# Spreading output products over the steps of a banded-attention kernel, with the early conv and value work and the first diagonals reordered

## The chip, the cores and the metric

One core of one Trainium2 chip. The metric is the device time of one execution in microseconds (us), lower is better. A run counts as slow if it is more than 1.5% above the fastest of its kernel; ratios use the other runs. The experiments ran on different chips, so compare kernels of different tables by their ratios.

Engine names as in the profile: PE is the matrix engine (TensorE), PEld its weight loads, DVE VectorE, ACT ScalarE, POOL GpSimd, SP the engine that issues most transfers (SPq is its queue).

## The reference

Inputs q, k, v are 8 x 8 x 576 x 64. Heads 0 to 3 attend to the last 32 positions, heads 4 to 7 to every fourth of the last 128. The result goes through a gated unit.

```python
scores = scale * np.matmul(q, k.transpose(0, 1, 3, 2))
mask_plain = (rel >= 0) & (rel < window)                       # heads 0..3
mask_dil = (rel >= 0) & (rel < window * dilation) & (rel % dilation == 0)
...
x = np.ascontiguousarray(attn_out.transpose(0, 2, 1, 3)).reshape(B, S, H * D)
...
for k in range(K):                                             # K = 5, causal
    gate_pre += conv_w[k][None, None, :] * xp[:, k:k + S, :]
gate = 1.0 / (1.0 + np.exp(-gate_pre))
val = x @ w_val
return (gate * val @ w_out).astype(np.float32)
```

## The kernel before

The loop runs over 32 head pairs, called steps; four make one batch, two make one group (one load of k and q). In a step PE does the scores (two halves of six products), ScalarE the exp, VectorE the mask, PE the product with the values (two halves), VectorE the normalisation. Into its waits PE gets work of earlier steps: the transposes of the next k and q (`trans_main`, `trans_rest`), the transposed attention result (`trans_x`), the gate's convolution as products with diagonal matrices (`conv`), the value products (`val`) and the output products (`out_tile`). The order is the program's: the schedule is manual. In the program `NCH` is 4 and `EARLY` 7; `xn` is the normalised attention result, `xT` its transpose, `k_b`, `q_b`, `vA` and `vB` are bf16 copies of loaded tiles. What matters of it, with `[...]` for cuts:

```python
    def normalize(i):            # after both halves of the attention product
        [...]
        nc.vector.reciprocal(out=rec[0:R], in_=av[:, :, :, D])
        nc.vector.tensor_tensor(out=dst, in0=av[:, :, :, 0:D], in1=rec..., op=ALU.mult)

    def out_tile(n):             # O4: four products of 512 columns
        [...]
        osb = out_pool.tile([128, Dm], FP32, name="osb")     # 4 buffers
        nc.scalar.mul(out=osb, in_=ps, mul=0.5)
        [... nc.sync.dma_start(out=out..., in_=osb...)]

    quota = [0.0]
    def slot_out():              # 1.125 credits a step, an output product for each
        quota[0] += 1.125
        while quota[0] >= 1 and outs:
            out_tile(outs.pop(0))
            quota[0] -= 1
    def slot_val():              # where no value product is due, an output product
        if vals:
            run_val()
        elif outs:
            out_tile(outs.pop(0))
            quota[0] -= 1

    for i in range(NP):
        [... loads]
        prep_v(i + 1)                                  # GpSimd: vA, vB
        [... cast(g2, "k"/"q", ..., nc.gpsimd)]        # GpSimd: k_b, q_b of a later group
        if i == NCH:                                   # the break at pair four
            after_x(i - 1); pop_conv(i + 1); pop_conv(i + 1)
            for _ in range(4): run_val()
            next_pair(i - 1); run_val(); run_val()
        scores(i, 0); scores(i, 1)
        [... after_x(i - 1), transposes, apply_mask(i, 0)]
        slot_val()
        pop_conv(...); apply_mask(i, 1); attn_v(i, 0)
        pop_conv(...); attn_v(i, 1); normalize(i)
        [... trans_rest]
        if i < NCH - 1: make_conv_diag(i + 1); warm(2)
        if i > NCH: slot_out()
        if vals: run_val()
```

An output product becomes due only when four value products more are done, that is in every second step, and then two or three at once; by then the credits for them have piled up. So from step 10 on two output products come after each even step (three in steps 12, 20 and 28) and none after an odd one. (`slot_val` spends credits in steps 5 to 7 alone, where no value product is due.) `warm(n)` are products of nothing, 512 columns, to keep PE busy.

The softmax here doesn't subtract the row's maximum and nothing guards it: scores larger than these inputs give would overflow.

Of the kernel before, what the change touches and what calls it, by code (L numbers as in the profile page):

```python
# [11 lines left out]
ALU = mybir.AluOpType  # L12
# [11 lines left out]
def kernel(  # L24
# [11 lines left out]
    nc = tc.nc  # L36

    B, H, S, D = q.shape
# [160 lines left out]
    def load_pair(g, a):  # L199
# [4 lines left out]
            load_rest(g, "q", nc.sync)  # L204
        load_v(g, a, a + 2)

    warm_in = consts.tile([1, 1], FP32, name="warm_in")
    nc.vector.memset(warm_in, 0.0)
    load_main(0, "k", 0, 2, nc.sync)
# [15 lines left out]
        out=ident, in_=ident, compare_op=ALU.not_equal, fill=1.0,  # L225
        base=0, pattern=[[-1, 128]], channel_multiplier=1,
    )
    nc.gpsimd.dma_start(out=conv_nat, in_=moe_conv_w)
    for kt in kTs:
        nc.vector.memset(kt[:, :, 0:KOFF], 0.0)  # L230
    for et in ets:
# [6 lines left out]
    def band(dst, pattern, base):  # L238
# [9 lines left out]
            channel_multiplier=1,  # L248
        )

    nc.gpsimd.memset(ident5, 0.0)
    nc.gpsimd.affine_select(
        out=ident5, in_=ident5, compare_op=ALU.not_equal, fill=1.0,
        base=0, pattern=[[-1, 8]], channel_multiplier=1,
    )
    band(mask_p[:, 1, :].rearrange("p (r t) -> p r t", r=4), [[1, 4], [4, 24]], 32)
    nc.gpsimd.tensor_copy(mask_p[:, 2:NB, :], mask_p[:, 1:2, :].to_broadcast([128, NB - 2, 96]))
    nc.gpsimd.tensor_copy(mask_p[:, 0, :], mask_p[:, 1, :])
# [31 lines left out]
    def finish_mask_d():  # L290
        mb = mask_d[:, 2 * TM:HB].rearrange("p (w t) -> p w t", w=2)
        nc.vector.tensor_scalar(
            out=par_i, in0=par_i, scalar1=1, scalar2=None, op0=ALU.bitwise_and)
        nc.vector.tensor_copy(same, par_i)
        nc.vector.tensor_tensor(
            out=mb, in0=mb, in1=same[:, :, None].to_broadcast([128, 2, TR]), op=ALU.mult)

    def setup_conv_w():
        ps = bank()
        for c in range(NCH):  # L300
            nc.tensor.transpose(
                out=ps[:, c * 8:c * 8 + K], in_=conv_nat[:, c * 128:(c + 1) * 128],
                identity=ident5[0:K, 0:K],
            )
        nc.scalar.copy(
            out=conv_w_sb, in_=ps[:, 0:NCH * 8].rearrange("p (c e) -> p c e", c=NCH)[:, :, 0:K])

    def make_conv_diag(c):
        nc.vector.tensor_tensor(
            out=conv_diag[:, c, :, :],  # L310
            in0=ident[:, None, :].to_broadcast([128, K, 128]),
            in1=conv_w_sb[:, c, :, None].to_broadcast([128, K, 128]),
            op=ALU.mult)
# [48 lines left out]
    def trans_rest(g):  # L362
        dil = g % 2
        t = grp_tiles[g]
        ps = bank_b()
        for z in range(2):
            nc.tensor.transpose(  # L367
                out=ps[:, 0, TM * z:TM * z + TM],
                in_=hi_bf16(t["rest"][:, 128 * z:128 * z + 128]), identity=ident)
        pv = ps[:, 0, 0:256].rearrange("p (z n) -> p z n", z=2)  # L370
        if not dil:
            if "qT" not in t:
                t["qT"] = qt_pool.tile([128, 2, DIL, T], BF16, name="qT")
            t["kT"] = kTs[(g // 2) % NKT]
            nc.vector.tensor_copy(t["kT"][:, :, KOFF + RM:KOFF + S], pv[:, :, 0:64])
            nc.vector.tensor_copy(
                t["qT"][:, :, :, TM:T], pv[:, :, 64:128].rearrange("p z (t r) -> p z r t", r=DIL))
        else:
            t["qB"] = qt_pool.tile([128, 4, 2, TR], BF16, name="qB")
            if "kB" not in t:  # L380
                t["kB"] = qt_pool.tile([128, 4, 64, 2], BF16, name="kB")
            nc.vector.tensor_copy(
                t["kB"][:, :, TM - TB:64, :],
                pv[:, :, 0:64].rearrange("p w (t h) -> p h t w", h=4))
            nc.vector.tensor_copy(
                t["qB"], pv[:, :, 64:128].rearrange("p w (t h) -> p h w t", h=4))
# [148 lines left out]
    def out_tile(n):  # L535
        ps = bank()
        for c in range(NCH):
            nc.tensor.matmul(  # L538
                out=ps, lhsT=y_all[:, c, 128 * n:128 * n + 128], rhs=w_out_b[:, c, :],
                start=(c == 0), stop=(c == NCH - 1),  # L540
            )
        osb = out_pool.tile([128, Dm], FP32, name="osb")
        nc.scalar.mul(out=osb, in_=ps, mul=0.5)  # L543
        p = 0
        while p < 128:
            f = 128 * n + p
            b, r, t = f // S, (f % S) // T, f % T
            w = min(128 - p, T - t)
            nc.sync.dma_start(
                out=out[b].rearrange("(t r) n -> r t n", r=4)[r, t:t + w, :],  # L550
                in_=osb[p:p + w, :])
            p += w
# [5 lines left out]
    def run_val():  # L558
        item = vals.pop(0)
        while item not in gates:  # L560
            conv(*convs.pop(0)[1])
        val(*item)
        done_val[0] += 1

        while HB * (done_val[0] // NCH) >= 128 * (done_out[0] + 1):
            outs.append(done_out[0])
            done_out[0] += 1

    def pop_conv(i):
        if convs and convs[0][0] < i:  # L570
            conv(*convs.pop(0)[1])

    def warm(n):
        for _ in range(n):
            nc.tensor.matmul(out=bank(), lhsT=junk[:, 0:128], rhs=junk, start=True, stop=True)
# [3 lines left out]
    def next_pair(i):  # L579

        j = i + 1
        g, z = j // 2, j % 2
        trans_main(g, "k", (z,))
        trans_main(g, "q", (z,))
        if z == 0:
            trans_rest(g)

    def after_x(i):
        b, c = pair_info(i)[0:2]
        trans_x(i)  # L590
        for G in range(2):
            convs.append((i + 1 + 0.5 * G, (b, c, G)))
        if c == NCH - 1:
            vals.extend((b, cc, G) for G in range(2) for cc in range(NCH))

    quota = [0.0]

    def slot_val():
        if vals:
            run_val()  # L600
        elif outs:
            out_tile(outs.pop(0))
            quota[0] -= 1

    def slot_out():
        quota[0] += 1.125
        while quota[0] >= 1 and outs:
            out_tile(outs.pop(0))
            quota[0] -= 1

    warm(8)
    cast(0, "k", 0, nc.vector)
    cast(0, "q", 0, nc.scalar)
    next_pair(-1)
    setup_conv_w()
    make_conv_diag(0)
    make_mask_d()
    make_perm()
    for i in range(NP):
        b, c, dil, g, a = pair_info(i)  # L620
        if i == 0:
            load_pair(2, 0)
        elif i == 1:
            load_pair(2, 2)
        elif i == 2:
            load_pair(3, 0)
        elif i == 3:
            load_pair(3, 2)
            load_group(4)
        if c % 2 == 0 and 5 <= g + 3 < 2 * B:  # L630
            load_group(g + 3)
        if i + 1 < NP:
            prep_v(i + 1)
        if i == 1:
            load_weight(w_val_b, moe_w_val)
        if i == 2:
            for name in ("k", "q"):
                cast(2, name, 0, nc.gpsimd)
        if i == 3:
            load_weight(w_out_b, moe_w_out)  # L640
            for name in ("k", "q"):
                cast(2, name, 2, nc.gpsimd)
        g2 = g + 2
        if 2 < g2 < 2 * B and g2 % 2 == 0:
            cast(g2, "k" if a == 0 else "q", 0, nc.gpsimd)
            cast(g2, "k" if a == 0 else "q", 2, nc.gpsimd)
        if i == NCH:
            after_x(i - 1)
            pop_conv(i + 1)
            pop_conv(i + 1)  # L650
            for _ in range(4):
                run_val()
            next_pair(i - 1)
            run_val()
            run_val()
        scores(i, 0)
        scores(i, 1)
        if i == 0:
            cast(0, "k", 2, nc.scalar)
            cast(0, "q", 2, nc.scalar)  # L660
        if i > 0 and i != NCH:
            after_x(i - 1)
        if NCH <= i < EARLY:
            next_pair(i)
        if i >= EARLY - 1 and g + 1 < 2 * B:
            trans_main(g + 1, "k" if a == 0 else "q")
        apply_mask(i, 0)
        if i < NCH:
            warm(3 if i == 0 else 1)
        slot_val()  # L670
        pop_conv(i if i >= NCH else i + 0.25)
        apply_mask(i, 1)
        attn_v(i, 0)
        if 0 < i < NCH - 1:
            next_pair(i)
        pop_conv(i + 0.5 if i >= NCH else i + 0.75)
        if i == 0:
            warm(1)
        attn_v(i, 1)
        normalize(i)  # L680
        if i == 0:
            next_pair(0)
            finish_mask_d()
        elif i >= EARLY - 1 and a == 0 and g + 1 < 2 * B:
            trans_rest(g + 1)
        if i < NCH - 1:
            make_conv_diag(i + 1)
            warm(2)
        if i > NCH:
            slot_out()  # L690
        if vals:
            run_val()
    pop_conv(NP)
# [38 lines left out]
```

## Time and profile before

Three runs: 192.55 us median (191.51 to 193.34). The profiled execution took 190.94 us, its span 189.2. A step ends where VectorE begins the reciprocal of the normalisation (L452); read from VectorE's timeline:

| end of step | 0 | 3 | 5 | 6 | 9 | 31 |
|---|---|---|---|---|---|---|
| us | 9.16 | 23.90 | 38.72 | 43.84 | 57.68 | 171.47 |

From step 9 on, two steps take 10.20 us (4.52 to 4.59 into an even step, 5.61 to 5.68 into an odd one; leaving out steps 13, 21 and 29, each behind a third output product, and the last two). How the clock, the transfers and their rate ran, in 40 slices of the span:

```profile
PEclk9999999999999999999999999999999999999999
DMA  5999999999998999999999969999780404021345
GB/s 153 257 300 309 263 253 297 319 230 341 304 201 257 335 295 213 287 316 284 246 294 322 263 159 268 328 283 242 249 280 0 111 3 151 19 77 40 110 111 166
```

A 9 is 90% or more. The transfers are busy until 140 us, and still move from 159 to 341 GB/s. The clock row says less about the first microseconds than it seems to: the trace's clock records begin at 5.00 us, and where there is none the view takes the clock as full. The start on VectorE (start, duration, instruction, in brackets the idle time before it):

```profile
4.58 0.43 DVE L181 CAST k_b<-k_nat 128x512 bf16<-128x512 f32 x1 [2.13 <-DMA k_nat<-in_k_dram]
...
6.95 0.91 DVE L309 TENSOR_TENSOR conv_diag<-ident,conv_w_sb 128x640 bf16<-128x640 bf16 x1
...
9.16 0.23 DVE L452 RECIPROCAL rec<-ps_sc 96x12 f32<-96x12 f32 x1 [0.46 <-PE ps_sc L441]
```

The first k is cast as soon as it lands; the first diagonal (L309) comes behind the first transposes.

### The profile page before, as it was taken

The page shows a single profiled execution, that of the slowest core. Times are in us where ns is not written, and L with a number is a line of the kernel's source. Part 1 is how long each engine was busy: PE and PEld are TensorE (multiplying, and loading weights), DVE is VectorE, ACT ScalarE, POOL GpSimd, SP SyncE. Part 2 cuts the span into 40 slices and gives each one's busy share as a digit, 9 for nine tenths or more (in the row PEclk, how much of TensorE's full clock was granted, in tenths as well). Part 3 has the DMA queues.
Part 4 walks back from the last instruction along what each step waited for, and adds up shares of the span by engine and source line. Part 5 has one row for each costly group of instructions (what it writes and reads, how often), then busy time and mean ns, then how long its engine had stood idle before and what let it go on. Part 6 is the DMA issues. An engine that isn't in the chain of part 4 may idle for free.

```text
span 189.2 us, 5191 instructions
## 1 busy us (share of the span) xinstructions
PE 166.2 (88%) x2039; PEld 119.4 (63%) x2057; DVE 118.8 (63%) x282; ACT 123.2 (65%) x218; POOL 41.0 (22%) x88
## 2 busy tenths in 40 slices
PE   6877769788898989899898989898999989899990
PEld 2455547466677665677676766766777766666650
DVE  3677637765576575765757764768667565756420
ACT  3756625788777676767787776767776877563341
POOL 7414420180090045003500350027030000000000
PEclk9999999999999999999999999999999999999999
DMA  5999999999998999999999969999780404021345
GB/s 153 257 300 309 263 253 297 319 230 341 304 201 257 335 295 213 287 316 284 246 294 322 263 159 268 328 283 242 249 280 0 111 3 151 19 77 40 110 111 166
DMA packets 62632, 42.28 MB, mean 223 GB/s; under 512 B 31371, under 2 KB 57995, under 8 KB 62608
## 3 DMA queue, kind: packets, MB, share of 16 engines
q1 hardware_dynamic: 60976, 40.57, 79.9%
q0 software_dynamic: 1088, 1.06, 3.3%
q8 instruction: 16, 0.26, 0.6%
q10 hardware_dynamic: 544, 0.33, 0.6%
q14 instruction: 8, 0.07, 0.1%
HBM read 33.56 MB, written 9.44 MB: 227 GB/s over the span
## 4 chain that ended last, share of the span: by engine, by line
PE 77%; DVE 15%; DMA 2%; ACT 2%; issue 2%; ACTq 0%; DVEq 0%
PE ps_bank L508 21%; PE ps_bank L538 16%; PE ps_bank L523 13%; DVE xn L457 8%; PE ps_bank L332 7%; PE ps_sc L441 7%; PE ps_sc L411 5%; PE ps_bank L469 3%; DVE rec L452 2%; DMA q_nat<-in_q_dram 2%; PE ps_bank L482 2%; PE ps_bank L476 2%; ACT et L414 1%; DVE xT L484 1%; PE ps_bank L367 1%
## 5 line engine op out<-in xcount | busy, mean ns | idle before, releaser
L508 PE MATMUL ps_bank<-xT,conv_diag 128*128 128x288 bf16 (+1 forms) x384 | 49.9, 266 | 2.0 <-DVE xT L484 2.0
L414 ACT ACTIVATE et<-ps_sc 128x576 bf16<-128x576 f32 x64 | 40.0, 650 | 14.6 <-PE ps_sc L411 13.4
L529 DVE SCALAR_TENSOR_TENSOR y_all<-gate,ps_bank 128x288 bf16<-128x288 bf16 x64 | 28.9, 451 | 20.2 <-PE ps_bank L523 17.8
L523 PE MATMUL ps_bank<-xT,w_val_b 128*128 128x288 bf16 x256 | 41.0, 286 | 0.2 <-DVE xT L484 0.2
L516 ACT ACTIVATE gate<-ps_bank 128x288 bf16<-128x288 f32 x64 | 26.5, 415 | 20.2 <-PE ps_bank L508 19.8
L508 PEld LDWEIGHTS <-conv_diag 128*128 128x128 bf16 x384 | 32.0, 97 | 8.9 <-issue 1.6
L543 ACT ACTIVATE osb<-ps_bank 128x512 f32<-128x512 f32 x36 | 21.6, 600 | 18.9 <-PE ps_bank L538 17.4
L538 PE MATMUL ps_bank<-w_out_b,y_all 128*128 128x512 bf16 x127 | 32.8, 379 | 0.9
L457 DVE TENSOR_TENSOR xn<-ps_sc,rec 96x768 bf16<-96x768 f32 (+1 forms) x32 | 30.6, 956 | 1.1
L523 PEld LDWEIGHTS <-w_val_b 128*128 128x128 bf16 x256 | 23.0, 98 | 7.2 <-issue 0.2
L181 POOL CAST k_b<-k_nat 128x512 bf16<-128x512 f32 x14 | 9.3, 687 | 82.4 <-DMA k_nat<-in_k_dram 57.4
L452 DVE RECIPROCAL rec<-ps_sc 96x12 f32<-96x12 f32 (+1 forms) x32 | 7.4, 231 | 25.3 <-PE ps_sc L441 25.3
L441 PEld LDWEIGHTS <-et 128*128 128x128 bf16 x384 | 19.8, 97 | 5.1 <-DVE et L423 2.4
L538 PEld LDWEIGHTS <-y_all 128*128 128x128 bf16 x144 | 13.4, 98 | 13.8 <-DVE y_all L529 1.3
L484 DVE COPY xT<-ps_bank 128x576 bf16<-128x576 bf16 x32 | 14.6, 458 | 11.4 <-PE ps_bank L482 6.5
L423 DVE TENSOR_TENSOR et<-et,mask_p 128x576 bf16<-128x576 bf16 x32 | 15.6, 494 | 0.5 <-ACT et L414 0.5
L423 DVE TENSOR_TENSOR et<-et,mask_d 128x576 bf16<-128x576 bf16 x32 | 15.6, 499 | 0.0
L188 POOL CAST vA<-v_st 128x512 bf16<-128x512 f32 x16 | 10.3, 641 | 16.9 <-DMA v_st<-in_v_dram 16.9
L411 PE MATMUL ps_sc<-qA,kA 64*128 64x128 bf16 x128 | 8.2, 219 | 6.3 <-DVE xn L457 4.8
L411 PE MATMUL ps_sc<-qT,kT 64*128 64x96 bf16 x192 | 8.2, 205 | 4.7 <-DVE xn L457 3.6
L441 PE MATMUL ps_sc<-vP,et 128*128 128x65 bf16 x192 | 11.3, 194 | 0.9 <-DVE et L423 0.8
L411 PEld LDWEIGHTS <-kA 64*128 64x128 bf16 x128 | 3.9, 94 | 11.4 <-DVE xn L457 5.9
(82 smaller groups left out, 190.6 us busy)
## 6 DMA issues: line engine op xcount, KB each, us to landing
k_nat<-in_k_dram SPq DMA_DIRECT2D x12, 512.0 KB, 5.6
q_nat<-in_q_dram SPq DMA_DIRECT2D x12, 512.0 KB, 6.4
vP<-in_v_dram SPq DMA_DIRECT2D x6, 768.0 KB, 8.4
v_st<-in_v_dram SPq DMA_DIRECT2D x6, 512.0 KB, 5.6
k_nat<-in_k_dram SPq DMA_DIRECT2D x8, 256.0 KB, 5.2
out_dram<-osb SPq DMA_DIRECT2D x8, 256.0 KB, 5.3
q_nat<-in_q_dram SPq DMA_DIRECT2D x7, 256.0 KB, 4.8
out_dram<-osb SPq DMA_DIRECT2D x8, 224.0 KB, 3.4
```

The lines of the kernel that those rows point to most:

```text
L411: nc.tensor.matmul(out=o, lhsT=lhsT, rhs=rhs, start=True, stop=True)
L414: nc.scalar.activation(out=e3, in_=ps[:, :, 0:HB], func=AF.Exp, scale=scale)
L423: nc.vector.tensor_tensor(out=e3, in0=e3, in1=m, op=ALU.mult)
L441: nc.tensor.matmul(out=ps[:, hf, x * AVS:x * AVS + D + 1], lhsT=et[:, hf, sl * HB + col:sl * HB + col + 128], rhs=rhs, start=True, stop=True)
L457: nc.vector.tensor_tensor(out=dst, in0=av[:, :, :, 0:D], in1=rec[0:R, :, :, None].to_broadcast([R, 2, 6, D]), op=ALU.mult)
L484: nc.vector.tensor_copy(xTs[b % NXT][:, c, :, 2:], pr)
L508: nc.tensor.matmul(out=ps[:, o * T:(o + n) * T], lhsT=conv_diag[:, c, K - 1 - m, :], rhs=xt[:, c, r:r + n, off:off + T], start=(idx == 0), ...
L516: nc.scalar.activation(out=gate, in_=ps[:, 0:HB], func=AF.Tanh, scale=0.5)
L523: nc.tensor.matmul(out=ps[:, 0:HB], lhsT=w_val_b[:, mc, c * 128:(c + 1) * 128], rhs=xt[:, mc, 2 * G:2 * G + 2, 2:], start=(mc == 0), stop= ...
L529: nc.vector.scalar_tensor_tensor(out=y_all[:, c, b * S + G * HB:b * S + (G + 1) * HB], in0=gates.pop((b, c, G)), scalar=1.0, in1=ps[:, 0:H ...
L538: nc.tensor.matmul(out=ps, lhsT=y_all[:, c, 128 * n:128 * n + 128], rhs=w_out_b[:, c, :], start=(c == 0), stop=(c == NCH - 1),)
L543: nc.scalar.mul(out=osb, in_=ps, mul=0.5)
```

## The change

Intent: (a) one output product in each step, so that each has enough PE work to cover its normalisation; (b) no burst of value products ahead of step 4: its work is spread like that of every other step, and the next pair's transposes go behind the first attention half; (c) the conv weights are transposed and the first three diagonals built at the very start, so that later steps need not. The diff, cut to its core:

```diff
+    nc.gpsimd.dma_start(out=conv_nat, in_=moe_conv_w)      # first of all, was after ident
 [...]
-        nc.scalar.copy(out=conv_w_sb, ...)
+        nc.vector.tensor_copy(conv_w_sb, ...)
 [... slot_val, slot_out, quota removed]
-    warm(8)
+    warm(5)
+    setup_conv_w()
+    make_conv_diag(0)
+    warm(3)
     cast(0, "k", 0, nc.vector)
     cast(0, "q", 0, nc.scalar)
-    next_pair(-1)
-    setup_conv_w()
-    make_conv_diag(0)
+    trans_main(0, "k", (0,))
+    make_conv_diag(1)
+    trans_main(0, "q", (0,))
+    trans_rest(0)
+    make_conv_diag(2)
 [... in the loop]
-        if i == NCH:
-            after_x(i - 1)
-            [... two convs, four vals, next_pair(i - 1), two vals]
-        if NCH <= i < EARLY:
-            next_pair(i)
-        if i >= EARLY - 1 and g + 1 < 2 * B:
+        if i >= EARLY and g + 1 < 2 * B:
             trans_main(g + 1, "k" if a == 0 else "q")
-        slot_val()
+        if vals:
+            run_val()
         attn_v(i, 0)
-        if 0 < i < NCH - 1:
+        if 0 < i < EARLY:
             next_pair(i)
+        if i == EARLY - 1:
+            trans_main(g + 1, "k")
 [... make_conv_diag(3) after step 0, none in the later steps]
-        if i > NCH:
-            slot_out()
+        for _ in range(2 if len(outs) > 2 else 1):
+            if outs:
+                out_tile(outs.pop(0))
```

More of the change, by code (lines that the diff above doesn't have):

```diff
@@ L227 @@
     )
-    nc.gpsimd.dma_start(out=conv_nat, in_=moe_conv_w)
+    nc.gpsimd.memset(ident5, 0.0)
+    nc.gpsimd.affine_select(
+        out=ident5, in_=ident5, compare_op=ALU.not_equal, fill=1.0,
+        base=0, pattern=[[-1, 8]], channel_multiplier=1,
+    )
     for kt in kTs:
@@ L249, in band @@
         )
-    nc.gpsimd.memset(ident5, 0.0)
-    nc.gpsimd.affine_select(
-        out=ident5, in_=ident5, compare_op=ALU.not_equal, fill=1.0,
-        base=0, pattern=[[-1, 8]], channel_multiplier=1,
-    )
     band(mask_p[:, 1, :].rearrange("p (r t) -> p r t", r=4), [[1, 4], [4, 24]], 32)
@@ L304, in setup_conv_w @@
             )
-        nc.scalar.copy(
-            out=conv_w_sb, in_=ps[:, 0:NCH * 8].rearrange("p (c e) -> p c e", c=NCH)[:, :, 0:K])
+        nc.vector.tensor_copy(
+            conv_w_sb, ps[:, 0:NCH * 8].rearrange("p (c e) -> p c e", c=NCH)[:, :, 0:K])
     def make_conv_diag(c):
@@ L594, in after_x @@
             vals.extend((b, cc, G) for G in range(2) for cc in range(NCH))
-    quota = [0.0]
-    def slot_val():
-        if vals:
-            run_val()
-        elif outs:
-            out_tile(outs.pop(0))
-            quota[0] -= 1
-    def slot_out():
-        quota[0] += 1.125
-        while quota[0] >= 1 and outs:
-            out_tile(outs.pop(0))
-            quota[0] -= 1
-    warm(8)
+    warm(5)
+    setup_conv_w()
+    make_conv_diag(0)
+    warm(3)
     cast(0, "k", 0, nc.vector)
     cast(0, "q", 0, nc.scalar)
-    next_pair(-1)
-    setup_conv_w()
-    make_conv_diag(0)
+    trans_main(0, "k", (0,))
[3 more added lines that the diff above has]
+    make_conv_diag(2)
     make_mask_d()
@@ L646 @@
             cast(g2, "k" if a == 0 else "q", 2, nc.gpsimd)
-        if i == NCH:
-            after_x(i - 1)
-            pop_conv(i + 1)
-            pop_conv(i + 1)
-            for _ in range(4):
-                run_val()
-            next_pair(i - 1)
-            run_val()
-            run_val()
         scores(i, 0)
@@ L660 @@
             cast(0, "q", 2, nc.scalar)
-        if i > 0 and i != NCH:
+        else:
             after_x(i - 1)
-        if NCH <= i < EARLY:
-            next_pair(i)
-        if i >= EARLY - 1 and g + 1 < 2 * B:
+        if i >= EARLY and g + 1 < 2 * B:
             trans_main(g + 1, "k" if a == 0 else "q")
@@ L682 @@
             next_pair(0)
+            make_conv_diag(3)
             finish_mask_d()
@@ L686 @@
         if i < NCH - 1:
-            make_conv_diag(i + 1)
             warm(2)
-        if i > NCH:
-            slot_out()
+        for _ in range(2 if len(outs) > 2 else 1):
+            if outs:
+                out_tile(outs.pop(0))
         if vals:
```

## The prediction

> **What bounds the kernel now.** I read the page first (engine shares, then the chain that ended last), then the chain in order of time through one pair of steady steps, then the waits, then the two stretches where the rhythm differs: the start, and the GpSimd casts around 37 us. A "step" is one head pair: scores, exp, mask, attention product, normalisation; there are 32, and the work of earlier pairs (transposes, gate convolution, value and output products) is threaded through them as filling.
>
> ```profile
> PE 166.2 (88%) x2039; PEld 119.4 (63%) x2057; DVE 118.8 (63%) x282; ACT 123.2 (65%) x218; POOL 41.0 (22%) x88
> ...
> PE 77%; DVE 15%; DMA 2%; ACT 2%; issue 2%; ACTq 0%; DVEq 0%
> ```
>
> PE is the engine that the end hangs on: 77% of the chain. What interests us is the 15% of VectorE: places where PE had run out of filling. The chain in order of time, steps 10 to 11:
>
> ```profile
> 62.33 1.67 PE ps_bank L538 x7
> 64.01 0.49 PE ps_bank L523 x4
> 64.50 0.37 PE ps_sc L411 x12
> ...
> 67.65 0.20 PE ps_sc L441 x6
> 67.86 0.02 issue
> 67.88 0.24 DVE rec L452
> 68.12 0.02 issue
> 68.15 0.97 DVE xn L457
> 69.11 0.05 issue
> 69.16 0.30 PE ps_sc L411 x6
> ```
>
> After the even step PE has two output products (L538) and a value product (L523) to do, and the scores (L411) run through without a wait. After the odd step it has one value product only: the chain leaves PE, goes through reciprocal and normalisation on VectorE, and returns 1.30 us later (67.86 to 69.16), since the second half of the scores needs the PSUM tile that the normalisation reads. The waits of PE:
>
> ```profile
> PE ps_sc L411 <- DVE xn L457: 8.4, 14, 0.7
> PE ps_sc L411 <- ACT et L414: 2.2, 3, 0.7
> PE ps_bank L508 <- DVE xT L484: 2.0, 4, 0.8
> ```
>
> In the timeline eleven of those 14 are the ends of the odd steps 9 to 29, 0.6 us each. The three waits on exp are steps 6, 7 and 8. So after step 9 the kernel is PE work plus 6.6 us of gaps. Before that, the end of step 3 (23.88 us) to the end of step 9 (57.65 us) is the stretch with the break at pair four. One row there matters later, from GpSimd's timeline:
>
> ```profile
> 37.07 1.64 POOL L181 CAST k_b<-k_nat 128x512 bf16<-128x512 f32 x2 [10.60 <-ACT kB L358]
> 38.66 0.61 POOL L188 CAST vA<-v_st 128x512 bf16<-128x512 f32 x1
> 39.22 0.40 POOL L191 CAST vB<-vB_st 128x256 bf16<-128x256 f32 x1
> ```
>
> The profile names an activation as releaser, but the program's waits on this cast are old ones except the load of k for group 4 (batch 2's first heads), which landed at 36.92 by the trace's semaphore records. It is a wait on DMA.
>
> **What the Trainium skill says.** "Perfetto Trace Analysis", Identifying the Most-Contended Engine: matmul busy share is a bad measure, since pipelined matmuls overlap in the trace; so I count PE time by the chain's pieces. The trace agrees: one L538 row lasts 379 ns, while four of them advance the chain by 0.86 us. "TensorE: Matmul & The Clock Gate", Wait — 56ns, not 53.3ns?: warm matmuls of 512 columns start every 215.7 ns; 0.86/4 = 0.215 us agrees, and granted clock is full in all 40 slices. The same page of trace analysis, Tensor Engine Instruction (MATMUL, LD_WEIGHTS), says that ScalarE, VectorE and GpSimd take their work strictly in order; the trace agrees, for the vA cast above starts only when the two k_b casts end although its own load had landed at 32.3. "DMA: Bandwidth & Descriptors", Specifications, puts HBM at about 358 GB/s per core; from 5 to 55 us my windows of 5 us show 258 to 316 GB/s with the DMA engines busy throughout, so I take it that early loads cannot come sooner.
>
> **The change part by part.** Instruction counts on PE are equal (the order listing shows 4109 rows in both, only moved), so everything is in the gaps.
>
> *Output products one per step.* Old order after an attention product: even steps O8 V4, odd steps V4 (O4 is one output tile's four matmuls, V4 one value product). New: every step O4 V4, O8 in steps 12, 20, 28. Needed cover: 1.30 us. New cover: O4 0.86 + V4 0.49 + first half of scores 0.18 to 0.25 = 1.53 to 1.60 us, plus 0.11 for the k/q rest transposes in even steps. That is over 1.30 in every step, by 0.2 to 0.4. Gaps removed: 11 x 0.6 = 6.6 us. Steps 9 to 31 last 171.44 - 57.65 = 113.8 us before, so 107.2 after; both do 25 output products in it.
>
> *No break, transposes behind the first half.* I rebuild steps 4 to 9 from the chain's pieces. Step 3 gains the transposes of the next pair (0.45 + 0.11), so it ends at about 23.88 + 0.56 = 24.4, plus what the start loses. Step 4: gap 1.30, second half of scores 0.27, x transposes 0.36, wait for xT 0.52, V4 0.49, attention 0.19, transposes 0.45, convolution 0.62, attention 0.19 = 4.4. Step 5 likewise 4.6 (no xT wait, one more convolution, rest transposes). So step 5 would end at 33.5 to 34.4. Step 6's first attention product would then be wanted at about 36.5 to 37.4. It reads vA and vB of pair 6, which GpSimd casts behind the k casts of group 4, which wait for a load landing at 36.9: vB is ready at 39.2 to 39.6 as before. This is the new wait, about 2 to 3 us. From there: remaining vB products 0.1, transposes 0.90, convolution 0.62, attention 0.19: step 6 ends at 41.3 (before: 43.8). Steps 7 to 9 are PE work, 4.83 each: rest transposes 0.11 or nothing, O4 0.86, V4 0.49, scores 0.37, x transposes 0.41, transposes 0.45, V4 0.49, two convolutions 1.24, two attention halves 0.38 = 4.7 to 4.8; the measured steps 10 and 11 give (10.26 - 0.6)/2 = 4.83. Step 9 ends at 41.3 + 14.5 = 55.8.
>
> *Start.* Building the diagonals earlier puts the weight copy and conv_diag ahead of the k cast on VectorE. conv_nat was issued at 1.53 and landed at 5.35; issued 0.7 earlier it lands near 4.6, the same time as k. Then transposes, copy (0.2) and conv_diag (0.82) come before the cast that ran at 4.58: the first pair's start is delayed by 0.4 to 1.3 us. In exchange diagonals 2 and 3 leave steps 1 and 2, where they ended just when VectorE was needed (16.70 against 16.72): nothing gained. But this loss ends in the wait of step 6, which hangs on a load and not on the start. On the path: 0.
>
> *Sum.* After the end of step 31 the tail is the same, except that one output product (0.86) is still owed. New end of step 31: 55.8 + 107.2 = 163.0, plus 0.86 = 163.9, against 171.44: 7.5 us. Time: 192.55 - 7.5 = 185.1 us, a ratio of 0.961.
>
> **The rivals.**
> First, no wait on the load: if vA is cast in time, step 6 ends 2 us sooner and the time is 183. Against it: GpSimd's order is the same in both builds, and up to 36.9 the loads are held up by the transfers ahead of them (the DMA row is full), not by compute.
> Second, DMA becomes the bound. A batch of four steps moves (33.56 MB read + 9.44 written - 2.1 of weights)/8 = 5.1 MB; at 4 x 4.83 = 19.3 us that asks 264 GB/s, near what the start shows at saturation. For it: the DMA row is at 9 until 140 us. Against it: in the steady part single slices reach 328 GB/s, loads are issued two to four steps before use, and the queue drains from 140 on. If it binds, half of the steady gain is lost: 188 to 189.
> Third, the gap does not close, because ScalarE or a bank takes the place of the normalisation: exp must now wait behind the copy of the output tile (0.60) in each step. ScalarE's load per step: two exp 1.3, copy 0.6, two gates 0.8, k/q copies 1.0 to 1.5 = 3.7 to 4.2 of 4.83. The first mask has slack of about 0.8 us before its attention product. If 0.2 us a step stays, 4 us are lost: 189.
> Fourth, the start's loss is not absorbed: 186.
>
> **Range and chances.** Centre 185.1. The steady gain (6.6) is counted directly; the early part (about 1 us after the new wait) is the looser term, with +2 if the wait is absent and -1 if the start shows. Runs of before spread by 0.9 us each way. Range 182.6 to 188.2. Two per cent is 188.7: faster 0.91, same 0.08, slower 0.01.
>
> **What would show each step.** PE's wait on xn from L411 should fall from 14 times to about 5, all before step 6, and no VectorE piece should stand in the chain between 60 and 160 us. A new row should appear: PE (L441) waiting on POOL vA or vB near 37 to 39.6 us, 2 us or so. Step 6 should end near 41.3 and steps thereafter take 4.8 us. In the first 10 us the k cast should start later than 4.58. Wrong would be: steps above 5 us after 60 us (then look whether PE waits for ACT et, or POOL for late loads), an early stretch that ends at 39 (the load was not the bound), or osb waiting for out_dram more than before's 1.5 us.

## The result, and the profile after

183.25 us median of four runs (182.80 to 186.42, the last of them slow), beside 192.94 us (191.51 to 193.49, four runs) for the kernel before. The ratio is 0.9501, 95% interval 0.943 to 0.957. (Ratios here and below are the mean time of one kernel's fast runs over that of the other's of the same rounds, so not quite the ratio of the medians quoted.) The profiled execution took 183.33 us with a span of 181.6: 7.6 us less than the span before.

Engines and chain of the page:

```profile
PE 166.6 (92%) x2057; PEld 119.9 (66%) x2057; DVE 119.3 (66%) x283; ACT 120.4 (66%) x217; POOL 42.8 (24%) x88
...
PE 85%; DVE 7%; POOL 3%; issue 2%; ACT 1%; POOLq 0%; ACTq 0%; DVEq 0%
```

PE's busy time is what it was (166.2 before); VectorE's share of the chain fell from 15% to 7%, and a new 3% belongs to GpSimd. What PE waited for (us in total, times, longest):

```profile
PE ps_sc L411 <- DVE xn L457: 2.5, 4, 0.7
...
PE ps_bank L301 <- POOL mask_d L246: 1.5, 1, 1.5
...
PE ps_sc L411 <- ACT et L414: 0.7, 1, 0.7
PE ps_sc L441 <- POOL vA L188: 0.6, 1, 0.6
...
PE ps_sc L441 <- POOL vB L191: 0.3, 1, 0.3
```

The wait on the normalisation went from 14 times to 4; the row for L301 is the wait for the conv weights in the start (the profile names a GpSimd instruction; the load landed at 5.19 us, and PE began at 5.33), those for vA and vB are the new wait in step 6. The chain through the steps that had the gap (compare the lines of the prediction from 62.33 to 69.16):

```profile
57.36 0.87 PE ps_bank L538 x4
58.23 0.49 PE ps_bank L523 x4
58.72 0.37 PE ps_sc L411 x12
...
62.12 0.86 PE ps_bank L538 x4
62.98 0.49 PE ps_bank L523 x4
63.47 0.37 PE ps_sc L411 x12
```

After the odd step 9 and after the even step 10 alike: the four matmuls of one output product, the four of a value product, then all twelve of the scores in one piece. Between 60 and 160 us the chain holds no piece of any engine but PE. The clock of the steps:

| end of step | 0 | 3 | 5 | 6 | 9 | 31 | 9 to 31 |
|---|---|---|---|---|---|---|---|
| before | 9.16 | 23.90 | 38.72 | 43.84 | 57.68 | 171.47 | 113.79 |
| after | 12.18 | 28.02 | 37.00 | 43.16 | 57.40 | 163.10 | 105.70 |
| predicted | 9.6 to 10.5 | 24.4 and the start's loss | 33.5 to 34.4 | 41.3 | 55.8 | 163.0 | 107.2 |

So practically all of the gain (8.1 of 8.4 us at the end of step 31) comes from the steady steps: two take 9.45 us (4.64 and 4.81) in place of 10.20. The whole early part, break and start together, brought 0.3 us. Two places there need an explanation. The start, on VectorE:

```profile
5.92 0.18 DVE L305 COPY conv_w_sb<-ps_bank 128x20 f32<-128x20 f32 x1 [3.48 <-PE ps_bank L301]
6.21 0.83 DVE L309 TENSOR_TENSOR conv_diag<-ident,conv_w_sb 128x640 bf16<-128x640 bf16 x1
6.95 0.43 DVE L181 CAST k_b<-k_nat 128x512 bf16<-128x512 f32 x1
...
12.18 0.23 DVE L452 RECIPROCAL rec<-ps_sc 96x12 f32<-96x12 f32 x1 [1.04 <-PE ps_sc L441]
```

The cast of k runs at 6.95 instead of 4.58, behind the weights' copy and the diagonal. And step 6, in the chain:

```profile
38.62 1.17 POOL k_b L181 x2
39.79 0.63 POOL vA L188
...
40.52 0.63 POOL vB L191
...
41.19 0.22 PE ps_sc L441 x2
41.42 0.89 PE ps_bank L332 x16
42.31 0.62 PE ps_bank L508 x6
```

PE's attention product of step 6 (L441) hangs on GpSimd's casts of vA and vB, and these stand behind the cast of group 4's k, which waited for its load. (The profile's timeline names PE's scores as its releaser, which ended at 38.59; the trace's semaphore records have the load landed at 38.48, and in the other profiles too this cast begins 0.14 or 0.15 us after the landing.) In the profile of the kernel before that cast began at 37.07, here at 38.62.

### The profile page after: what moved, and what is told of

Its sections match the earlier page's. It is cut to its first block, busy times and chain, and to the rows that moved or that the text cites. A ratio compares the mean times of both kernels' runs of the same rounds, so it can differ in the third digit from the quotient of the medians.

```text
span 181.6 us, 5203 instructions
## 1 busy us (share of the span) xinstructions
PE 166.6 (92%) x2057; PEld 119.9 (66%) x2057; DVE 119.3 (66%) x283; ACT 120.4 (66%) x217; POOL 42.8 (24%) x88
## 4 chain that ended last, share of the span: by engine, by line
PE 85%; DVE 7%; POOL 3%; issue 2%; ACT 1%; POOLq 0%; ACTq 0%; DVEq 0%
PE ps_bank L508 22%; PE ps_bank L538 17%; PE ps_bank L523 16%; PE ps_bank L332 8%; PE ps_sc L441 7%; PE ps_sc L411 6%; PE ps_bank L469 3%; DVE xn L457 3%; PE ps_bank L482 2%; PE ps_bank L476 2%; DVE xT L484 1%; PE ps_bank L575 1%; PE ps_bank L367 1%; DVE conv_diag L309 1%; DVE rec L452 1%
## 5 line engine op out<-in xcount | busy, mean ns | idle before, releaser
L414 ACT ACTIVATE et<-ps_sc 128x576 bf16<-128x576 f32 x64 | 38.7, 648 | 6.6 <-PE ps_sc L411 4.2
L523 PE MATMUL ps_bank<-xT,w_val_b 128*128 128x288 bf16 x256 | 41.8, 286 | 0.4 <-DVE xT L484 0.4
L538 PE MATMUL ps_bank<-w_out_b,y_all 128*128 128x512 bf16 x144 | 36.4, 379 | 0.0
L441 PEld LDWEIGHTS <-et 128*128 128x128 bf16 x384 | 20.4, 98 | 5.8 <-DVE et L423 2.3
L538 PEld LDWEIGHTS <-y_all 128*128 128x128 bf16 x144 | 12.5, 97 | 10.9 <-DVE y_all L529 0.9
L423 DVE TENSOR_TENSOR et<-et,mask_p 128x576 bf16<-128x576 bf16 x32 | 16.3, 512 | 0.2 <-ACT et L414 0.2
L188 POOL CAST vA<-v_st 128x512 bf16<-128x512 f32 x16 | 12.1, 755 | 14.2 <-PE ps_sc L411 9.3
L423 DVE TENSOR_TENSOR et<-et,mask_d 128x576 bf16<-128x576 bf16 x32 | 14.9, 470 | 0.0
L441 PE MATMUL ps_sc<-vP,et 128*128 128x65 bf16 x192 | 11.6, 197 | 0.1
L347 ACT COPY kT<-ps_bank 128x1024 bf16<-128x1024 bf16 (+1 forms) x10 | 8.5, 848 | 4.6 <-PE ps_bank L332 4.6
L575 PE MATMUL ps_bank<-junk 128*128 128x512 bf16 x21 | 8.8, 520 | 1.6 <-DVE junk L221 1.6
L441 PE MATMUL ps_sc<-vA,et 128*128 128x65 bf16 x128 | 9.3, 194 | 0.6 <-POOL vA L188 0.6
```

The costliest lines, as they stand in the source:

```text
L414: nc.scalar.activation(out=e3, in_=ps[:, :, 0:HB], func=AF.Exp, scale=scale)
L423: nc.vector.tensor_tensor(out=e3, in0=e3, in1=m, op=ALU.mult)
L441: nc.tensor.matmul(out=ps[:, hf, x * AVS:x * AVS + D + 1], lhsT=et[:, hf, sl * HB + col:sl * HB + col + 128], rhs=rhs, start=True, stop=True)
L523: nc.tensor.matmul(out=ps[:, 0:HB], lhsT=w_val_b[:, mc, c * 128:(c + 1) * 128], rhs=xt[:, mc, 2 * G:2 * G + 2, 2:], start=(mc == 0), stop= ...
L538: nc.tensor.matmul(out=ps, lhsT=y_all[:, c, 128 * n:128 * n + 128], rhs=w_out_b[:, c, :], start=(c == 0), stop=(c == NCH - 1),)
```

## The experiments

Theory: the gain is PE idle time behind the odd steps, filled; the break's removal and the new start are worth nothing, because what they change ends in step 6's wait on a load. Rivals: the break gave part of the gain; the gain is not idle time but fewer collisions; the start costs in the end.

### The parts one by one

`spread_only`: the kernel before with (a) alone.

```diff
-        elif outs:                       # in slot_val
-            out_tile(outs.pop(0))
-            quota[0] -= 1
-        if i > NCH:
-            slot_out()
+        for _ in range(2 if len(outs) > 2 else 1):
+            if outs:
+                out_tile(outs.pop(0))
```

> The kernel before with only the output products spread, one per step; break and start as before. Theory (gaps at the ends of odd steps are the steady loss): steps 9 to 31 take about 105.7 us instead of 113.8, no step after 13 is over 4.9 us except the three with two products, and the time is about 184.5 us, a ratio to before of 0.955 to 0.965. Rival (the gain came from the removed break, or the steady part is held by transfers): steps stay above 5 us on average, ratio above 0.98.

`nobreak_only`: the kernel before with (b) alone, that is the changed kernel with the old start and with `slot_out` in place of the new loop.

> The changed kernel with the old start and the output products bunched in even steps: the break's removal alone. Theory (step 6 waits for the cast behind the load of group 4, which lands near 36.9 to 38.5): step 6 ends at 41.5 to 43, step 9 at 57 to 58.5 as before, gain 0 to 1 us, ratio 0.995 to 1.0. Rival (the break itself cost time): step 9 ends 2 to 4 us sooner, ratio 0.98 to 0.99.

`start_only`: the kernel before with (c) alone, that is the first block of the diff above and the lines on `make_conv_diag`.

> The kernel before with only the start of the changed one (weights and diagonals first). Theory (the new start costs, and nothing in the old order takes the loss up, as step 6's first attention product came 3 us after its operands): the first reciprocal at 12.2 instead of 9.2 us, the end of step 9 later by 3 to 3.6, time 3 us longer, ratio 1.015 to 1.02. Rival (the loads take it up here too): first reciprocal 3 us later but step 9 within 1 us of before, ratio 1.0 to 1.005.

`after_old_start`: (a) and (b), the changed kernel without (c).

> The changed kernel with the old start. Theory (in the changed kernel the loss of the start ends in step 6's wait for GpSimd's casts): the first reciprocal is back at 9.2 us, the wait of the attention product on vA or vB grows from 0.9 to about 3 us, step 6 ends where it did (41.5 to 43.1), and the time is that of the changed kernel less 0 to 1.5 us (ratio to before 0.942 to 0.95). Rival (the loss goes through to the end): step 6 ends near 40 and the time is 3 us below the changed kernel, ratio 0.935.

These four shared seven runs of the kernel before, 193.46 us median:

| | median us | ratio, 95% interval | end of step 0 | step 9 | step 31 | 9 to 31 |
|---|---|---|---|---|---|---|
| spread_only (a) | 184.77 | 0.953, 0.942 to 0.965 | 9.17 | 59.09 | 164.49 | 105.40 |
| nobreak_only (b) | 193.21 | 0.993, 0.982 to 1.005 | 9.01 | 60.92 | 174.72 | 113.80 |
| start_only (c) | 195.53 | 1.015, 1.006 to 1.023 | 12.24 | 61.35 | 175.54 | 114.19 |
| after_old_start (a, b) | 184.91 | 0.959, 0.951 to 0.967 | 8.97 | 57.20 | 163.90 | 106.70 |

(The profile of nobreak_only fell in a slow run; use its ratio, which leaves slow runs out.) What follows: (a) alone gives the whole steady gain, 8.4 us from step 9 to 31, and a time that cannot be told from the full change. (b) alone is within the noise, and so is (b) on top of (a) (184.91 beside 184.77). (c) alone loses 3.1 us at step 0 and carries them to the end, where nothing early absorbs them. With (b) in place the loss does not show: after_old_start starts 3.2 us sooner than the changed kernel and is only 0.2 us sooner at step 6. (Its 106.70 has about 1 us more in steps 16, 17 and 27 than the changed kernel; these were not followed up.)

### Is the gap worth what its wait records?

The prediction took 0.6 us for each gap, the wait that the profile records; the steps got shorter by 0.75 per two. So products of nothing were put into the kernel before, after odd or after even steps.

```diff
             slot_out()
+        if i >= 9 and i % 2 == 1:      # even2: i % 2 == 0
+            warm(2)                     # odd6: warm(6)
```

> The kernel before with two products of nothing (512 columns, 0.43 us by the row of the output products) after every odd step from 9 on, where PE has one value product as cover. My theory: they run inside the gap in which PE waits for the normalisation, so they are free: steps 9 to 31 last 113.8 us as before (up to 0.3 more), the time is the same within its noise. Rival (the gap is no idle PE time, but PE work counted otherwise, and the gain of the change came from something else, such as the smaller burst on PSUM banks or ScalarE): every product costs its time, 11 x 0.43 = 4.7 us more.

> The kernel before with the same two products after every even step from 10 on, where PE already has two output products and a value product as cover. My theory: no gap is there to take them up, so each costs its time: 11 x 0.43 = 4.7 us more, steps 9 to 31 near 118.5 us. Rival (there is slack in even steps too): less than 1 us more.

> The kernel before with six products of nothing (1.29 us) after every odd step from 9 on: more than the gap holds, so what is over measures the gap. Theory A (the gap is worth 0.75 us, as two steps fell from 10.20 to 9.45 us in the changed kernel): 1.29 - 0.75 = 0.54 us a step over, 11 x 0.54 = 5.9 us more, and the interval from the end of an odd step to the end of the next even one goes from 4.52 to near 5.06. Theory B (the gap is worth the 0.6 us that the wait records): 0.69 us over, 7.6 us more, the interval near 5.21.

Beside the kernel before at 192.94 us (seven runs of the same rounds):

| | median us | ratio, 95% interval | 9 to 31 | against 113.79 | odd to even | even to odd |
|---|---|---|---|---|---|---|
| before | 192.94 | | 113.79 | | 4.52, 4.59 | 5.61 to 5.68 |
| two after odd steps | 193.44 | 1.007, 0.999 to 1.015 | 114.05 | +0.26 | 4.53 to 4.66 | 5.61 to 5.79 |
| two after even steps | 197.52 | 1.027, 1.016 to 1.039 | 118.89 | +5.10 | 4.53 to 4.64 | 6.04 to 6.16 |
| six after odd steps | 200.63 | 1.046, 1.038 to 1.054 | 119.75 | +5.96 | 5.07 to 5.13 | 5.61 to 5.67 |

(The columns "odd to even" and "even to odd" are the intervals from the end of one step to that of the next; intervals into steps 13, 21 and 29, which have an extra output product, and into the last two are left out.) The same two products are free after an odd step and cost their full 0.43 us after an even one. Six take 1.29 us and lengthen the interval by 0.54: the gap took up 0.75, as theory A had it, not 0.6. PE's wait in the first two of them:

```profile
PE ps_sc L411 <- DVE xn L457: 3.6, 14, 0.7
```

```profile
PE ps_sc L411 <- DVE xn L457: 8.4, 14, 0.7
```

With the products after the odd steps (first fence) there are still 14 waits, but 4.8 us less of them, 11 x 0.44; after the even steps the wait is that of the kernel before. Where the 0.15 between 0.6 and 0.75 goes can mostly be read from the prediction's own lines: behind the gap the six products of the second half advance the chain by 0.30 (69.16), in an unbroken run twelve take 0.37 (64.50), which is 0.18 for six. So the six products behind a wait take 0.12 longer, in time that no wait records; 0.03 stays unexplained.

### What holds step 6

after_old_start, from the end of its wait of 3.1 us on vA; first the chain, then the engines in windows of a microsecond (busy time of PE, PEld, DVE, ACT and POOL with their numbers of instructions, then the granted clock as a share of full, the transfers' share and GB/s):

```profile
38.82 0.57 POOL vA L188
...
39.43 0.61 PE ps_sc L441 x6
40.05 1.71 PE ps_bank L332 x16
41.75 0.99 PE ps_bank L508 x6
```

```profile
38.00:39.00 1.00, 0.00 (x0) 0.00 (x0) 0.00 (x0) 0.00 (x0) 1.00 (x3) 0.99 1.35 241
39.00:40.00 1.00, 0.57 (x8) 0.49 (x8) 0.00 (x0) 0.00 (x0) 1.00 (x3) 0.50 1.25 209
40.00:41.00 1.00, 1.00 (x12) 1.00 (x10) 0.00 (x0) 0.49 (x2) 1.00 (x3) 0.50 1.31 223
41.00:42.00 1.00, 1.00 (x11) 0.91 (x9) 0.00 (x0) 0.81 (x3) 0.74 (x2) 0.50 0.80 137
42.00:43.00 1.00, 1.00 (x14) 0.82 (x13) 0.03 (x1) 0.82 (x1) 0.00 (x0) 0.81 0.25 60
```

The sixteen transposes take 1.71 us, in the changed kernel 0.89. The Trainium skill, "TensorE: Matmul & The Clock Gate", Part 1, What's actually happening, says that an idle window of about 3.4 us puts the array on half its clock, and about as long a busy one brings it back. The trace agrees in kind: PE stopped at 36.31, its clock records have 0.50 from 38.97 to 42.39 (3.42 us), and the wait ended at 39.43, so the clock fell 2.7 us into it. So the old start waited longer and then ran slower, which ate its lead. Test: fill that wait with products of nothing.

```diff
         apply_mask(i, 1)
+        if i == EARLY - 1:
+            warm(12)
         attn_v(i, 0)
```

> The changed kernel with the old start and 12 products of nothing (128 columns of weights, 512 columns) put into step 6 just ahead of its first attention product, where PE waited 3.1 us. Theory (the wait lowers the clock that the throttle grants, and 16 transposes then take 1.71 us instead of 0.89, and six convolution products 0.99 instead of 0.62): with 2.6 us of filling in the wait, the transposes take 0.9 us again, step 6 ends near 41.8 instead of 42.97, and the whole is about 1.1 us shorter. Rival (the transposes are slow because their input comes late, not because of the clock): the 1.71 us stay, and step 6 ends at 42.9 or later.

The other three change what step 6 waits for. `after_early_v` is the changed kernel with pair 6's vA and vB cast in step 4, ahead of the k cast; `after_old_start_early_v` the same on the old start; `late_group4` has in addition the transposes of group 4's k in step 7 instead of 6.

```diff
-        if i + 1 < NP:
+        if i + 1 < NP and i + 1 != 2 * NCH - 2:
             prep_v(i + 1)
+        if i == NCH:
+            prep_v(2 * NCH - 2)
 [... late_group4 only:]
-            trans_main(g + 1, "k" if a == 0 else "q")
+            trans_main(g + 1, "k" if a == 0 or i == EARLY else "q")
-        if i == EARLY - 1:
-            trans_main(g + 1, "k")
+        if i == EARLY:
+            trans_main(g + 1, "q")
+            trans_rest(g + 1)
-        elif i >= EARLY - 1 and a == 0 and g + 1 < 2 * B:
+        elif i > EARLY and a == 0 and g + 1 < 2 * B:
             trans_rest(g + 1)
```

> The changed kernel with one edit: GpSimd casts the values of pair 6 in step 4, ahead of its k and q casts for group 4, instead of behind the k casts. My theory (step 6 of the changed kernel waits for these casts, which stand behind a cast that waits for a load landing near 38.5 us): PE's two waits on vA and vB (0.6 and 0.3 us) disappear, step 6 ends near 42.3 instead of 43.16, and the whole is about 0.9 us shorter, 182.3 us. Rival A (the load of k itself holds step 6, by the transposes of group 4's k that stand behind the first attention half): the wait only moves to those transposes, step 6 still ends at 43. Rival B (later loads hold the steps 7 to 9): step 6 ends sooner but step 9 still ends at 57.4.

> The changed kernel with the old start, and with pair 6's values cast in step 4. With the old start alone step 6 waited 3.1 us for vA and ended at 42.97. My theory: the attention product no longer waits, but the transposes of group 4's k, which follow it, wait for the cast of k that ends near 39.8; so step 6 ends near 41.5 if the clock stays up, and near 42.5 if an idle of about 3 us lowers it as it did with the old start alone. Gain over the old start alone 0.4 to 1.4 us, and step 9 ends at 56 to 57. Rival (GpSimd's order is all there is to the wait): the 3.1 us go away altogether, step 6 ends near 39.9 and step 9 near 54.3.

> Old start, early cast of pair 6's values, and the transposes of group 4's k moved from step 6 into step 7, its q and rest behind them: nothing in step 6 reads a late load. My theory (the load of group 4's k, landing near 38 us, is what bounds the early part, so its first reader should stand as late as possible): step 6 ends near 38, step 7 near 44 after a wait of 1 to 1.5 us, step 9 near 54 to 55, total 179.5 to 181. Rival (the loads after it come at their own rate too, so the time is only handed on to the next load): step 8 or 9 waits for q of group 4 or k of group 5, step 9 ends at 56.5 or later, and the total is within 0.9 us of the changed kernel with early values.

Beside 192.80 us for the kernel before:

| | median us | ratio, 95% interval | step 5 | step 6 | step 9 | step 14 | step 31 |
|---|---|---|---|---|---|---|---|
| after (earlier rounds) | 183.25 | 0.950, 0.943 to 0.957 | 37.00 | 43.16 | 57.40 | 81.78 | 163.10 |
| after_early_v | 182.09 | 0.950, 0.945 to 0.954 | 36.98 | 41.95 | 56.31 | 80.69 | 161.88 |
| after_old_start (earlier) | 184.91 | 0.959, 0.951 to 0.967 | 33.27 | 42.97 | 57.20 | 81.59 | 163.90 |
| after_old_start_warm | 182.79 | 0.953, 0.948 to 0.958 | 33.66 | 42.36 | 56.59 | 81.78 | 162.93 |
| after_old_start_early_v | 182.51 | 0.950, 0.942 to 0.957 | 35.45 | 41.31 | 57.21 | 83.66 | 164.89 |
| late_group4 | 183.36 | 0.958, 0.949 to 0.966 | 33.40 | 37.93 | 54.69 | 81.33 | 162.91 |

after_early_v: both waits on vA and vB are gone, step 6 ends 1.2 us sooner, and the 1.2 are still there at the end. My theory of GpSimd's order held (expected 0.9). The load landed 0.74 us sooner in this run, but that is not it: PE's transposes of that k began at 40.50, later than the 39.79 at which the cast ended in the changed kernel. The ratios, 0.950 for both, do not show so small a gain.

after_old_start_warm: the chain goes, with the products of nothing at L575,

```profile
36.70 1.52 PE ps_bank L575 x7
38.27 1.17 POOL k_b L181 x2
...
40.61 0.89 PE ps_bank L332 x16
41.51 0.62 PE ps_bank L508 x6
```

and the transposes take 0.89 again. From the start of the k cast to the end of step 6 it took 4.09 us (38.27 to 42.36), against 5.32 without the filling (37.65 to 42.97). That is the 1.2 of the clock, and idle PE cost it. It shows over the runs too: the mean clock of the four runs was 0.994 to 0.998 with the filling and 0.978 to 0.991 without. The end of step 6 gained only half, since in this run the load came 0.6 later. (The ratios, 0.953 and 0.959, overlap.)

after_old_start_early_v is the unclear one: its profile fell in a slow run, with a half clock around 30 us that stretched step 4 to 6.16 us (4.34 in after_old_start) without any wait of PE above 0.74 us just ahead. Its step 7 then waited 1.4 us for the small rest load of q. So this profile shows the next load as the bound of step 7, but not how much the early cast is worth; its ratio says that it is no worse than the changed kernel.

late_group4: step 6 ended at 37.93 and step 9 2.7 us sooner than in the changed kernel, as expected; but I had the total wrong (179.5 to 181 expected, 183.36 came). The lead was gone in step 14, not in 8 or 9 as the rival had it. ScalarE and the transfer queue there:

```profile
78.30 0.60 ACT L543 ACTIVATE osb<-ps_bank 128x512 f32<-128x512 f32 x1 [3.66 <-DMA out_dram<-osb]
```

```profile
62.06 2.76 SPq L549 DMA_DIRECT2D out_dram<-osb  x4
64.91 0.40 SPq L115 DMA_DIRECT2D k_nat<-in_k_dram  x1
65.41 0.55 SPq L115 DMA_DIRECT2D q_nat<-in_q_dram  x1
66.84 0.63 SPq L127 DMA_DIRECT2D qk_rest<-in_k_dram  x1
67.56 1.57 SPq L127 DMA_DIRECT2D qk_rest<-in_q_dram  x1
69.22 0.56 SPq L148 DMA_DIRECT2D vP<-in_v_dram  x1
69.87 7.57 SPq L549 DMA_DIRECT2D out_dram<-osb  x4
```

The stores of the output (L549) share SP's queue with the loads. From 64.91 on five loads are issued, 1.9 MB together by the sizes of the page's issue table, and the next stores stand behind them: the first was issued at 69.87, its issue took 4.94 us, and it landed at 77.81. ScalarE had no free buffer until one of the stores had landed. Step 14 was stretched in after_old_start_early_v (6.55 us) and after_old_start_warm (5.45) too. If it is a matter of buffers, two more should end it:

```diff
-    out_pool = ctx.enter_context(tc.tile_pool(name="osb", bufs=4))
+    out_pool = ctx.enter_context(tc.tile_pool(name="osb", bufs=6))
```

> The late_group4 version with six buffers for the output tile instead of four. In late_group4 the gain of the early steps (2.7 us at step 9) was given back in step 14, where ScalarE waited 3.7 us for an output buffer whose store had been issued behind five loads, and PE 1.9 us for ScalarE. Theory: with two more buffers that wait falls away, step 14 ends near 79.2 instead of 81.3, and the total is 180.5 to 181.5, below every version so far. Rival (DMA as a whole is behind at this point): the wait moves to a load (a cast on GpSimd, or the next step's transposes), step 14 or 16 still ends where late_group4 has it, and the total stays near 183.

179.89 us median (179.14 to 180.96), ratio 0.936 (0.929 to 0.943), the best of all; its interval and that of the changed kernel meet at 0.943. Step 14 took 4.64 us in place of 6.81, although the same store landed only 0.5 us sooner (77.30); so the theory held, not the rival. That the loads ahead of them delay the stores is read from the order of the queue and was not tried by itself. Not all of it is the buffers' doing: in this run group 4's q was cast at 39.80 instead of 41.28, before any output tile could have waited for a buffer, so that step 7 took 5.35 instead of 7.33. Of the 4.0 us between the two profiles at step 31, 2.2 are step 14 and 2.0 are step 7, with small differences elsewhere. The medians differ by 3.5 us, so how much of it the buffers are worth over all runs is not shown. The page of this run:

```profile
PE 165.1 (93%) x2057; PEld 119.1 (67%) x2057; DVE 118.8 (67%) x282; ACT 120.7 (68%) x218; POOL 41.7 (23%) x88
...
PEclk9999999999999999999999999999999999999999
```

PE is busy for 93% of a span of 177.4 us, and the clock row shows a 9, 90% or more, in all 40 slices.

## Why the prediction was right or wrong

The time was right: 185.1 predicted with a range of 182.6 to 188.2, and 183.25 came. Its end of step 31, 163.0, was met within 0.1 us. But two of its terms were off by about 1.5 us each, in opposite directions: the right total is partly luck.

*Steady steps: mechanism right, size too small.* "Gaps removed: 11 x 0.6 = 6.6 us" is the mis-sized term. Spreading alone took 8.4 us out of steps 9 to 31, the whole change 8.1, and the six products of nothing measured the gap at 0.75. The prediction took for its worth what the wait records; the slower products behind the wait (0.12 us) come on top. The cover argument itself (1.53 us or more against 1.30) held in every step, with no piece of VectorE in the chain from 60 to 160 us, and xn waits fell from 14 to 4, where about 5 were expected.

*Early part: the place of the wait right, its hour wrong.* "Step 6 ends at 41.3" was 43.16. The waits on vA and vB came, but at 40.4 to 41.2 us, since the cast of k ahead of them began at 38.62 and not at 37.07. The prediction took the landing of group 4's k, 36.92 in the one profile that it had, as fixed ("early loads cannot come sooner"). That landing was an exception. The three kernels with products of nothing are the kernel before up to the end of step 9, and in their profiles the same load landed at 38.47, 38.53 and 38.73; over the other thirteen profiles it landed at 37.51 to 38.74. So the 38.48 of the changed kernel is the usual hour, and the early gain was 0.3 us in place of 1.9. The new start does issue this load later (33.05 against 31.72 with the old start on the same kernel, 32.92 in start_only against 31.82), but this does not show in the landing: with the new start it was 37.74 to 38.71. The time from issue to landing varied from 4.81 to 6.79 us. Two smaller slips: 24.4, 4.4, 4.6 and a loss of 0.4 to 1.3 make 33.8 to 34.7 for step 5, not 33.5 to 34.4; and the 10.26 us of its check are steps 11 and 12 (10 and 11 took 10.20). The rebuilt steps themselves were good: with the old start, step 5 ended at 33.27.

*Start: undersized.* "Delayed by 0.4 to 1.3 us" was 3.0 us. The conv weights were issued at 1.35, only 0.2 sooner, because GpSimd's queue was held up for 0.8 us first, and landed at 5.19 instead of "near 4.6". Four transposes (0.57), the copy and the diagonal then moved the k cast by 2.4 us. The other 0.65 us came between the cast and the first reciprocal: the one product of nothing between the two attention halves took 0.43 where it took 0.22 before, and three ahead of them 1.40, so PE was at half its speed there. The trace's clock records agree: the first of them, with full clock, begins at 12.05 us in the changed kernel and at 5.00 in the kernel before (11.89 to 13.89 in the three profiles with the new start, 4.37 to 7.47 in the eleven with the old one). The old start gives PE eight products of nothing without a break from 1.56 to about 5 us; the new one leaves it idle for 1.46 us from 3.87 on, waiting for the conv weights. That this idle time is what kept the clock low is likely, but was not tried. "On the path: 0" held for most of it: start_only loses 3.1 us at step 0 and 4.1 at step 31, but on top of (a) and (b) the new start costs nothing that the medians show (183.25 against 184.91 without it). One reason is that the old start pays for the longer wait with a half clock. The prediction had the clock in neither place.

*Rivals.* The first (no wait on the load, 183) fell, though the time is its number: the wait is there. The second (DMA binds) fell for the changed kernel, whose steps stay at 4.64 to 4.81 us; in late_group4 stores and loads did bind, in step 14, but through the output buffers, and two more buffers ended it. The third (another wait takes the gap's place) fell. The fourth (the start's loss shows) fell for the changed kernel; it holds in start_only, without (a) and (b). ScalarE's wait for output buffers, named as a sign of trouble above 1.5 us, was 2.2, and late_group4 made it a bound at 6.1 (2.5 with six buffers).

*What is open.* The medians differ by 9.7 us, the profiles by 7.6. In two of the six profiled kernels that keep the break (spread_only and the two products after odd steps) step 4 took 11.82 us instead of 10.16, with the clock lowered for some of it. Both half clocks lasted 3.41 us and followed a wait of 1.32 us that all six have. If unprofiled runs of the kernel before have this too, the break costs more on average than its profile says; that is argued, not shown.

## What to carry to other kernels

Where a loop alternates between too much filling and too little, look at the short side only: here spreading the same work evenly was worth the whole gap, and the gap was worth more than the wait that is recorded. A few products of nothing put into a gap measure it: here they were free up to its size. A load's landing in one profile is a single draw: before a forecast rests on it, look at more profiles of the same code. Before work is pulled forward into an early step, find the load that bounds it and place its first reader late; and when that is done, expect the next shared resource, here the buffers of stores that queue behind loads.

## What the Trainium skill lacked or had wrong

- "TensorE: Matmul & The Clock Gate", What's actually happening: right in kind, and worth 1.2 us here (16 transposes 1.71 us instead of 0.89). The wait was 3.1 us, which is below the 3.4 stated, and the clock fell 2.7 us into it. In three profiles (spread_only, before_fill_odd2, after_old_start_early_v) the clock was also halved for 3.41 us without any wait above 1.32 us in the 4 us before; what made it is not shown.
- "Perfetto Trace Analysis", Optimization Strategy, tells to look for the gaps; it lacks that a gap on PE costs more than its recorded wait: 0.75 us against 0.6, measured with six products of 1.29 us of which 0.54 showed.
- "DMA: Bandwidth & Descriptors", Anatomy of one DMA, gives about 2.0 us of fixed cost for a transfer issued by GpSimd; the 10 KB of conv weights took 3.8 us from issue to landing, in both kernels, while other loads kept the engines busy.
